# Attention followed by a gated Fourier convolution: head pairs row-tiled, e stationary in 128-column slices, transforms folded twice, casting weight loads

## The chip, the cores and the metric

One Trainium2 chip, one core. The metric is device time in microseconds (us) of the whole launch. The kernel before took 622.55 us (median of 2 runs, 620.84 to 624.26). Engines are called PE (TensorE; PEld is its weight load), DVE (VectorE), ACT (ScalarE), POOL (GpSimd) and SP. A run over 1.5% above the fastest of its kernel counts as slow; only fast runs are compared.

## The reference, cut to what matters

```python
# q, k, v: (8, 12, 448, 64); w_proj: (768, 2304); filter_fft: (448, 768); w_out: (768, 768)
scores = q @ k.T / 8
attn   = exp(scores - m) / (sum(exp(scores - m)) + exp(-m) + 1e-9)     # equals exp(s) / (sum exp(s) + 1), but for the 1e-9
x      = (attn @ v) as (8, 448, 768)
x1, x2, x3 = split(x @ w_proj)
y      = x1 * irfft(rfft(x2, axis=1) * rfft(filter_fft, axis=0)) * x3
out    = y @ w_out
```

Both kernels run the attention of batch b + 1 in the same stretch as the dense part (projections, transform, output) of batch b, so that TensorE has dense matmuls to do while ACT computes exps. The transforms are matmuls with sine and cosine tables.

## The kernel before

One PSUM pool has two buffers each of four tags: `tr` for transposes, `hy` for dense tiles, `sc` for scores, `op` for the attention output. The buffers of one tag form a ring: a new tile gets the buffer of the tile that many places before it, once that one has been read. The parts:

```python
psum = ctx.enter_context(tc.tile_pool(name="psum", bufs=2, space=bass.MemoryType.PSUM))

def attn_pair_scores(A, hp):
    qtps = psum.tile([128, 512], F32, name="qtps", tag="tr")     # q of two heads, transposed; then k
    # ... copies: qT; kTA = k of head 0 over zeros, kTB = zeros over k of head 1
    for i in range(NST):
        for u, kT in enumerate((kTA, kTB)):
            scps = psum.tile([SP, S], F32, name="scps", tag="sc")
            nc.tensor.matmul(scps, kT[:, i * SP : (i + 1) * SP], qT[:, :])
            e = etp.tile([SP, S], BF16, name="ET", tag="ET")
            nc.scalar.activation(e, scps, AF.Exp, scale=SCALE, bias=exp_bias[:SP, 0:1])

def attn_pair_O(A, hp, et):
    for u in range(2):
        oph = psum.tile([SP, NST, DH + 1], F32, name="oph", tag="op")     # two buffers
        # ... 16 matmuls: e in 112-column slices stationary, v and a column of ones moving
        nc.vector.tensor_scalar_add(rec, oph[:, :, DH], 1.0)              # normalisation on DVE
        nc.vector.reciprocal(rec, rec)
        nc.vector.tensor_tensor(xb[:, :, h, :], oph[:, :, 0:DH], ..., op=ALU.mult)

def attn_finish(A):                              # once a batch, behind all six pairs
    for dt in range(NDT):
        xtps = psum.tile([128, 512], F32, name="xtps", tag="tr")
        # ... 4 transposes of xb, one copy to xT[:, dt, :]

# per pair: attn_pair_scores, one chunk of the dense part of the batch before, attn_pair_O
```

The softmax here doesn't subtract the row's maximum and nothing guards it: scores larger than these inputs give would overflow.

## Time and profile before

| | kernel before |
|---|---|
| time | 622.55 us |
| period of the loop (first x1 matmul of a batch to that of the next) | 67.85 us |
| first x1 matmul of batch 0 (the start) | 82.5 us |
| last dense part, to the end | 49.7 us |
| mean granted TensorE clock | 0.988 |

The prediction has 91 us for the start, as it takes two periods of 67.85 us from batch 2; but the first period takes 76.4. It reads the period, the busy times and the groups. One more view matters for what follows: what TensorE does where a pair ends. The columns of a timeline are start (us), length (us), engine, line, operation, count, and in brackets the idle time ahead of it with what ended it.

```profile
244.04 3.76 PE L345 MATMUL pps<-xT,wproj_bf 128*128 128x448 bf16 x19
247.63 1.80 PE L291 MATMUL oph<-vext,ET 112*112 112x65 bf16 x32
249.28 0.36 PE L245 MATMUL qtps<-ident_bf,qf 112*128 112x112 bf16 x4
```

Both heads' outputs run as one row of 32 matmuls, and the next pair's transposes follow at once. No brackets: nothing on TensorE waits for DVE here, although DVE normalises each head. The list of TensorE's waits says nearly the same of the whole run; its columns are us in total, times, and the longest.

```profile
PE fps L156 <- ACT tpages L121: 37.1, 4, 18.1
...
PE xtps L315 <- DVE xb L301: 1.0, 1, 1.0
```

The largest is the sine tables, at the start. For `xb`, the normalised output, it waited once, 1.0 us.

### The profile page before, as it was taken

To read this page: it belongs to the slowest core of one execution; us is meant where nothing else is said; L and a number is where in the kernel's file an instruction comes from. 1 tells how busy PE (TensorE), PEld (TensorE's weight loads), DVE (VectorE), ACT (ScalarE), POOL (GpSimd) and SP (SyncE) were. 2 spreads that over 40 slices of the span, in tenths; PEclk is the share of its full clock that TensorE was granted. 3 is DMA by queue.
4 is the path that set the end of the run, shared out by engine and by line. 5 is a ranking of instruction groups with operands and counts; after the bars stand their busy time and mean duration, and the time that the engine had idled before them with its cause. 6 is when DMAs were issued, how large, how long until landed. Compare 5 with 4: busy or idle time off the path is not lost.

```text
span 615.7 us, 10809 instructions
## 1 busy us (share of the span) xinstructions
PE 541.6 (88%) x4336; PEld 367.8 (60%) x4336; DVE 347.8 (56%) x929; ACT 278.1 (45%) x527; POOL 145.6 (24%) x237
## 2 busy tenths in 40 slices
PE   0127889999999899989999899989999999989977
PEld 0014665766667575757667566757576666757544
DVE  4743545475464935394656746393647546493572
ACT  0106775436436255536355453545453643735112
POOL 3533263033211522033301531052212300100000
PEclk9997898999999999999999999999999999999999
DMA  9999097029900985069900991088901920002002
GB/s 235 235 209 204 1 92 46 1 16 98 113 1 2 79 124 25 2 40 97 91 1 1 91 124 12 1 55 117 56 1 13 101 69 1 1 1 90 2 1 89
DMA packets 137810, 39.04 MB, mean 63 GB/s; under 512 B 131424, under 2 KB 131424, under 8 KB 137760
## 3 DMA queue, kind: packets, MB, share of 16 engines
q0 software_dynamic: 130560, 16.52, 46.6%
q1 hardware_dynamic: 7200, 21.83, 12.0%
q8 instruction: 34, 0.56, 0.4%
q14 instruction: 16, 0.13, 0.1%
HBM read 43.84 MB, written 11.01 MB: 89 GB/s over the span
## 4 chain that ended last, share of the span: by engine, by line
PE 78%; DVE 11%; DMA 6%; ACT 4%; issue 1%; DVEq 0%
PE scps L271 14%; PE oph L291 12%; PE ops L444 10%; PE pps L360 10%; PE pps L345 9%; PE pps L331 9%; PE cps L424 4%; ACT ET L277 4%; DMA w<-in_moe_w_proj_dram 4%; PE xr L378 3%; PE xi L387 3%; DMA f<-in_moe_filter_fft_dram 3%; DVE t L399 2%; PE ktps L255 1%; DVE t L408 1%; PE xtps L315 1%
## 5 line engine op out<-in xcount | busy, mean ns | idle before, releaser
L277 ACT ACTIVATE ET<-scps,exp_bias 112x448 bf16<-112x448 f32 x384 | 217.3, 635 | 214.9 <-PE scps L271 209.3
L291 PEld LDWEIGHTS <-ET 112*112 112x112 bf16 x1536 | 98.0, 133 | 18.1 <-issue 5.3
L291 PE MATMUL oph<-vext,ET 112*112 112x65 bf16 x1536 | 101.8, 217 | 0.7
L299 DVE TENSOR_SCALAR rec<-oph 112x4 f32<-112x4 f32 x96 | 15.2, 158 | 137.4 <-PE oph L291 136.3
L262 POOL MEMSET kTA<- 64x448 bf16 x48 | 22.5, 469 | 236.8 <-PE scps L271 223.0
L444 PE MATMUL ops<-wout_bf,yT 128*112 128x384 bf16 x384 | 74.3, 326 | 0.0
L271 PE MATMUL scps<-qT,kTB 128*112 128x448 bf16 x192 | 69.0, 359 | 4.9 <-DVE kTB L265 2.7
L360 PE MATMUL pps<-wproj_bf,xT 128*112 128x384 bf16 x384 | 72.9, 326 | 0.0
L271 PE MATMUL scps<-qT,kTA 128*112 128x448 bf16 x192 | 69.4, 361 | 3.4 <-DVE kTA L264 1.6
L331 PE MATMUL pps<-xT,wproj_bf 128*128 128x448 bf16 x288 | 71.8, 354 | 0.1
L345 PE MATMUL pps<-xT,wproj_bf 128*128 128x448 bf16 x288 | 64.6, 352 | 0.0
L444 PEld LDWEIGHTS <-yT 128*112 128x112 bf16 x384 | 48.5, 129 | 15.9 <-issue 1.8
L360 PEld LDWEIGHTS <-xT 128*112 128x112 bf16 x384 | 48.6, 129 | 15.7 <-issue 1.5
L424 PE MATMUL cps<-bt,yhat 128*128 128x448 bf16 x192 | 44.9, 351 | 9.2 <-DVE t L408 9.0
L367 ACT CAST x2n<-pps 112x384 bf16<-112x384 f32 x64 | 29.9, 480 | 37.6 <-PE pps L360 37.6
L451 ACT COPY osb<-ops 112x384 f32<-112x384 f32 x64 | 29.8, 480 | 37.1 <-PE ops L444 26.4
L338 DVE CAST x1T<-pps 128x448 bf16<-128x448 f32 x48 | 29.9, 624 | 28.9 <-PE pps L331 28.6
L352 DVE CAST x3T<-pps 128x448 bf16<-128x448 f32 x48 | 30.0, 624 | 23.4 <-PE pps L345 22.3
L345 PEld LDWEIGHTS <-wproj_bf 128*128 128x128 bf16 x288 | 27.9, 98 | 24.8 <-issue 2.8
L301 DVE TENSOR_TENSOR xb<-oph,rec 112x256 bf16<-112x256 f32 x96 | 40.1, 418 | 1.9
L331 PEld LDWEIGHTS <-wproj_bf 128*128 128x128 bf16 x288 | 27.5, 98 | 20.9 <-issue 3.0
L227 POOL DMA_DIRECT2D vext<-in_v_dram x32 | 31.4, 986 | 32.4 <-PE xtps L315 28.2
(68 smaller groups left out, 632.2 us busy)
## 6 DMA issues: line engine op xcount, KB each, us to landing
out_dram<-osb SPq DMA_DIRECT2D x32, 336.0 KB, 2.7
w<-in_moe_w_proj_dram SPq DMA_DIRECT2D x12, 576.0 KB, 7.0
qf<-in_q_dram POOLq DMA_DIRECT2D x32, 168.0 KB, 5.4
kf<-in_k_dram POOLq DMA_DIRECT2D x32, 168.0 KB, 5.2
vext<-in_v_dram POOLq DMA_DIRECT2D x32, 168.0 KB, 6.1
wo<-in_moe_w_out_dram SPq DMA_DIRECT2D x6, 384.0 KB, 5.7
f<-in_moe_filter_fft_dram SPq DMA_DIRECT2D x4, 336.0 KB, 4.6
```

Source lines behind the costliest of these rows:

```text
L227: nc.gpsimd.dma_start(vext[:, st, :, 0:DH], v[b, :, st * SP : (st + 1) * SP, :].rearrange("h p d -> p h d"),)
L271: nc.tensor.matmul(scps, kT[:, i * SP : (i + 1) * SP], qT[:, :],)
L277: nc.scalar.activation(e, scps, AF.Exp, scale=SCALE, bias=exp_bias[:SP, 0:1])
L291: nc.tensor.matmul(oph[:, j, :], et[u][i][:, j * SP : (j + 1) * SP], vext[:, i, h, :], start=(i == 0), stop=(i == NST - 1),)
L301: nc.vector.tensor_tensor(xb[:, :, h, :], oph[:, :, 0:DH], rec[:].unsqueeze(2).to_broadcast([SP, NST, DH]), op=ALU.mult,)
L331: nc.tensor.matmul(pps, wproj_bf[:, kt, dt * 128 : (dt + 1) * 128], xT[:, kt, :], start=(kt == 0), stop=(kt == NDT - 1),)
L338: nc.vector.tensor_copy(hb["x1T"][:, dt, :], pps)
L345: nc.tensor.matmul(pps, wproj_bf[:, kt, 2 * D + dt * 128 : 2 * D + (dt + 1) * 128], xT[:, kt, :], start=(kt == 0), stop=(kt == NDT - 1),)
L352: nc.vector.tensor_copy(hb["x3T"][:, dt, :], pps)
L360: nc.tensor.matmul(pps[:SP, :DCH], xT[:, kt, st * SP : (st + 1) * SP], wproj_bf[:, kt, D + ch * DCH : D + (ch + 1) * DCH], start=(kt == 0) ...
L424: nc.tensor.matmul(cps, yhat[:W, pg, dt * 128 : (dt + 1) * 128], bt[:W, pg, :], start=(pg == 0), stop=(pg == 3),)
L444: nc.tensor.matmul(ops_[:SP, :DCH], yT[:, dt, st * SP : (st + 1) * SP], wout_bf[:, dt, ch * DCH : (ch + 1) * DCH], start=(dt == 0), stop=( ...
```

## The change

The intent is fewer and cheaper TensorE instructions, and an earlier start. Row-tiled means that the scores of two heads, 64 rows each, use the two halves of TensorE's rows, where each head took all 128, half of them zeros. Folded means that sums and differences of mirrored positions and of the two halves of the sequence are formed first, so that the tables shrink. The core of the diff, cut (`...`):

```diff
+    psc = ctx.enter_context(tc.tile_pool(name="psc", bufs=2, space=bass.MemoryType.PSUM))
+    pop = ctx.enter_context(tc.tile_pool(name="pop", bufs=1, space=bass.MemoryType.PSUM))
+    phy = ctx.enter_context(tc.tile_pool(name="phy", bufs=3, space=bass.MemoryType.PSUM))
...
+Q0 = [0, 128, 256, 320]
...  # scores: k of head u lies in rows 64u to 64u+63, no zeros; one exp for both heads
+        tps = phy.tile([128, 512], F32, name="tps", tag="hy")       # transposes of q and k
...
+            sc = psc.tile([SP, 2, 512], F32, name="sc")
+            for u in range(2):
+                r = slice(64 * u, 64 * u + 64)
+                nc.tensor.matmul(
+                    sc[:, u, 0:S], qkT[r, S + j * SP : S + (j + 1) * SP], qkT[r, 0:S]
+                )
+            nc.scalar.activation(e, sc[:, :, 0:S], AF.Exp, scale=SCALE)
...
+    def attn_pair_out(A, hp, et):
+        for u in range(2):
+            op = pop.tile([128, NST, DH + 1], F32, name="op")
...  # 16 matmuls, stationary et[j][:, u, Q0[t] : Q0[t] + 128]; then the same three DVE steps into xb
+        tps = phy.tile([128, 512], F32, name="xps", tag="hy")       # transposes of x, now pair by pair
+        for t in range(NST):
+            nc.tensor.transpose(
+                tb[:, Q0[t] : Q0[t] + 128], xb[:, t, 2 * hp : 2 * hp + 2, :], ident_bf
+            )
+        nc.vector.tensor_copy(xT[:, hp, 0:S], tb[:, 0:S])
...  # dense part: folds of xT on DVE; spectrum 8 matmuls in place of 32; inverse 24 of 224 columns in
...  # place of 24 of 448; every dense tile is phy.tile(..., tag="hy")
-            w32 = stmp_w.tile([128, WCH], F32, name="w32", tag="w32")
-            nc.sync.dma_start(w32, moe_w_proj[...])
-            nc.vector.tensor_copy(wproj_bf[...], w32)
+            nc.gpsimd.dma_start(wproj_bf[:, kt, cs], moe_w_proj[kt * 128 : (kt + 1) * 128, cs])
...
+            for hp in range(NHP):
+                et = attn_pair_scores(N, hp)
+                chunks[hp]()
+                attn_pair_out(N, hp, et)
```

All transposes and all dense tiles now share one ring of three PSUM buffers (`hy`). The x transposes moved from the end of a batch to the end of each pair.

## The prediction

The sum of the period: 51.9 us of work and 6 of waits, so 58, and 525 in all. ACT's "about 40" is 33.5 + 10.2 less a term for the exps of 896 columns. The range of 36 us to each side had one term more, for the mode switches, and the three that are left give 26 in quadrature. Rival 1: the switches cost more than row tiling saves. A mode switch is a change between full-height and row-tiled matmuls on TensorE; as the kernel before has none, the 0.1 us for each is the estimate from the 352 and 189 ns named with it. The "fast load" is the one of 98 ns.

> **What bounds the kernel now.** I read the page's busy shares first, then the chain that ended last in order of time, then the groups of instructions with shapes kept apart, then busy times by stretch, and last the timeline of TensorE inside one batch.
>
> ```profile
> PE 541.6 (88%) x4336; PEld 367.8 (60%) x4336; DVE 347.8 (56%) x929; ACT 278.1 (45%) x527; POOL 145.6 (24%) x237
> ...
> PE 78%; DVE 11%; DMA 6%; ACT 4%; issue 1%; DVEq 0%
> ```
>
> TensorE is busy 88% and carries 78% of the chain. The next view, busy time by stretch, is cut where the projection of x1 recurs in the chain:
>
> ```profile
> 234.01:301.87 67.86, 65.38 (x538) 44.47 (x536) 39.53 (x108) 33.46 (x65) 17.36 (x28) 1.00 0.61 52
> 301.87:369.73 67.86, 65.39 (x538) 44.48 (x536) 39.51 (x108) 33.47 (x65) 17.37 (x28) 1.00 0.57 52
> ```
>
> The columns are the stretch, its length, busy us of PE, PEld, DVE, ACT, POOL, then clock, DMA share and GB/s. One batch takes 67.85 us, PE is busy 65.4 of them at full clock, DVE 39.5 and ACT 33.5. The first x1 matmul of a batch starts at 226.76 us and of the last at 566.03 in the timeline, five periods apart, so the span splits into 91 us before the loop (226.76 minus two periods), 7 x 67.85 = 475 in it, and 49.7 for the last dense part. The launch time of 622.55 is 6.9 over the profiled span.
>
> Busy time hides what a matmul costs, so I price by start-to-start time. These are lines of the chain (start, us, what):
>
> ```profile
> 247.80 1.64 PE oph L291 x32
> ...
> 256.80 3.92 PE pps L360 x24
> ...
> 312.06 3.59 PE pps L345 x19
> ```
>
> 1.64/32 = 51 ns for an attention-output matmul (65 columns streamed), 3.92/24 = 163 ns for 384 columns, 3.59/19 = 189 ns for 448. From the last two, a column costs 0.41 ns with 3 to 5 ns beside; 65 columns should then cost 30 ns, yet they cost 51. The reason is in the groups:
>
> ```profile
> L277 ACT ACTIVATE ET<-scps,exp_bias 112x448 bf16<-112x448 f32 x384 | 217.3, 635 | 214.9 <-PE scps L271 209.3 <-PE oph L291 3.2 <-PE qtps L245 0.5
> ...
> L291 PEld LDWEIGHTS <-ET 112*112 112x112 bf16 x1536 | 98.0, 133 | 18.1 <-issue 5.3 <-ACT ET L277 2.4 <-DVE xb L301 0.9
> ...
> L315 PEld LDWEIGHTS <-xb 112*128 112x128 bf16 x192 | 12.4, 98 | 8.0 <-issue 4.3 <-DVE xb L301 1.1
> ```
>
> A weight load of 112 columns takes 133 ns, one of 128 columns only 98: the wider is faster, and the output matmuls are set by their slow loads. The first line shows ACT waiting for scores, not the other way round.
>
> The budget of a batch by these prices: x1 and x3 72 x 189 ns = 13.6 us; x2 and the output 96 x 163 = 15.6; spectrum 32 x 163 = 5.2; inverse 24 x 189 = 4.5; scores 48 x 189 = 9.1; 72 transposes at 49 ns (four in 0.19 to 0.20 us by the timeline) = 3.5; attention output 192 x 51 = 9.8. Sum 61.3; the other 6.5 are waits (some 2.5 us of idle PE) and small gaps where scores mix with dense matmuls.
>
> [...] Eight exps of 448 run in 4.50 us in the timeline, 0.56 us each[...]. [...] The trace: 550 ns for a 384-column product with PSUM, 350 for a 384-column subtraction in SBUF.
>
> **The change part by part, per batch on TensorE.**
> - Scores: each head contracts 64 rows in place of 128 with zeros. If a pair runs side by side, 24 pairs x 0.19 = 4.6 us in place of 9.1: -4.5. The zero-padded copies of k (a split copy on DVE, two POOL memsets) go as well.
> - Switching: scores of one j are paced by ACT, and dense matmuls fill between, so I expect two mode switches per j, 48 a batch. A recorded 448-column matmul lasts 352 ns and the next starts 189 after it, so up to 0.16 us lies behind the last column; I estimate 0.1 us exposed for each: +4.8.
> - Attention output: e in 128-column slices gets the fast load, so streaming binds, 192 x 31 ns = 6.0 in place of 9.8: -3.8.
> - Forward transform folded twice: 8 matmuls in place of 32: -3.9. Projection of x2 keeps its 48 (now on folded x, 113-column weights hidden behind 384 columns).
> - Inverse: 24 matmuls of 224 columns at about 96 ns in place of 24 x 189: -2.2.
> - Transposes of x take 128 columns: +0.2.
>
> Sum: 61.3 - 4.5 + 4.8 - 3.8 - 3.9 - 2.2 + 0.2 = 51.9, of which 4.8 are switches. The waits I leave at 6: the single buffer for the attention output makes head 1 wait for the normalisation of head 0 (0.16 + 0.18 + 0.42 us of DVE), and three PSUM buffers serve all dense tiles, but DVE has less to do. Period 58 us, 10 less, 69 us over seven batches.
>
> ACT: [...] copies of x1, the transform and the inverse come over (some 8 x 0.48 + 12 x 0.53 = 10.2), so ACT goes from 33.5 to about 40. DVE: the 16 + 8 products and sums of the spectrum (8 x 0.56 on SBUF + 8 x 0.35 = 7.3 against 11.6), the x1 copies and the k copies go, twelve folds of about 0.5 us come: 6.1; in all about 36 against 39.5. Both stay under 58.
>
> Before the loop: now 91 us. Scores start at 51.3 us, behind a serial chain of sine tables and their transposes, with the DMA moving 192 to 239 GB/s in the first 60 us. After the change q, k and v of batch 0 go first, in thirds, so attention 0 runs from some 17 us on under the weight loads. What then binds is bytes: the weights (21.8 MB on the hardware queue less 11.0 of output = 10.8 MB, 46 us at 235 GB/s) and two batches of q, k, v (2.06 MB each as written, at about 120 GB/s when the queue is full in steady state, 17 us each), of which v of batch 1 can come late: about 70 us. -21.
>
> The last dense part: -6.1 of transform matmuls, and the spectrum's waits for DVE partly replaced by waits for folds: about 43 in place of 49.7.
>
> Total: 70 + 7 x 58 + 43 = 519, plus 6.9: 526 us; I say 525.
>
> **The rivals.**
> 1. [...]
> 2. **ACT becomes the bound.** It goes to 40 of 58 us, and it holds both the exps and most PSUM evacuations, in order. [...] Against it: 30% slack, and three buffers of 1 us each.
> 3. **The casting loads are slower or later than thought.** All loads now go through POOL's queue, at 0.93 us of issue for each q, k, v load. The next batch's loads have a full second buffer, so in the loop they are hidden, as the DMA share of 0.6 suggests. At the start it could cost 15 us: loop from 85 us, total 540.
> 4. **Hidden anyway.** If TensorE were not the bound the removed matmuls would be worth nothing. Its 65.4 busy of 67.85 us speaks against it.
>
> **Range and chances.** The terms: [...] waits 6 +- 2.5, so +-18; start +-14; attention output at 31 or 40 ns, +12 at worst. Added in quadrature, about 36 to each side for 8 in 10: 490 to 562. Over 2% faster needs less than 610, beyond everything listed: 0.96. Within 2%: 0.025. Slower: 0.015.
>
> **What would show it.** The period between first x1 matmuls of batches near 58. Two score matmuls of one j starting within a few ns of each other, 24 pairs a batch; if they start 189 apart, the side-by-side step is wrong. [...] Attention-output matmuls 30 to 32 ns apart and their loads near 98 ns; 50 would say that streaming does not bind. Spectrum 8 matmuls, inverse 96 ns each. Exps near 1.0 us long, 24 a batch; ACT busy near 40. First x1 matmul of batch 0 near 70 us. The prediction is wrong if the period stays over 63, with ACT's queue or the switches naming what ended PE's idle time, or if the loop starts after 85 us.

The trace after has these for the prices above. Exps of 896 columns last 0.917 us and follow each other at 0.81 (of 448 columns before: 0.633 and 0.54), and ACT is busy 36.1 us a batch. From the start of an x3 matmul to that of a score pair 297 ns pass, and 326 from a pair to the next x3 matmul (medians, 190 to 635 us), where two full-height matmuls of 448 columns start 189 apart: 0.11 us more ahead of a pair and 0.14 behind it. The x2 matmuls start 163 ns apart, as with 112-column weights before (162), so their 113-column loads of 135 ns are hidden. Products of 768 columns in SBUF take 0.55 to 0.56 us.

## The result, and the profile after

The changed kernel took 680.59 us (median of 2 runs, 679.89 to 681.28) against 622.55: ratio 1.0931, 95% interval 1.0854 to 1.1007, all runs fast. Here and below, a ratio is the mean time of one kernel's fast runs over that of the other's fast runs of the same rounds, so it is not quite the ratio of the medians that I quote. It is slower by 58 us where I had said 98 faster.

| | before | predicted | after |
|---|---|---|---|
| time | 622.55 | 525 | 680.59 |
| start | 82.5 (91 in the prediction) | 70 | 87.9 |
| period | 67.85 | 58 | 78.4 |
| last dense part | 49.7 | 43 | 42.6 |
| clock | 0.988 | not considered | 0.904 |

(After: the first x1 matmuls of batches 0 and 7 start at 87.9 and 636.8 us, seven periods apart; the span is 679.3.) Start and loop are the miss; the last dense part is right. (The clock's record in this run has no entry before 87.4 us, so the 9s at its head say nothing: the 384-column matmuls from 82.34 us on start 0.32 us apart, twice the 163 ns of full clock.) First the page: busy shares, the clock in 40 slices, and the shares of the chain that ended last.

```profile
PE 521.3 (77%) x4112; PEld 315.9 (46%) x4112; DVE 271.3 (40%) x769; ACT 299.2 (44%) x492; POOL 131.3 (19%) x213
...
PEclk9999987889969899698978899698987998688989
...
PE 57%; DVE 15%; ACT 14%; DMA 6%; POOL 4%; issue 3%; ACTq 0%; DVEq 0%; POOLq 0%
```

No engine is full: PE fell from 88% to 77% in a longer span, and nothing else passed 46%. That is the picture of engines that wait for each other. The clock has 6s and 7s all along the loop. One period by engine (the same columns as in the prediction's view by stretch), then the waits of TensorE over the whole run:

```profile
324.77:403.30 78.53, 62.43 (x510) 37.46 (x508) 32.13 (x91) 36.14 (x60) 12.31 (x20) 0.89 0.52 44
```

```profile
PE op L268 <- DVE xb L278: 64.2, 41, 8.0
PE xps L287 <- DVE xb L278: 45.2, 48, 1.6
```

TensorE is idle 16 of 78.5 us of the period. 109 of the 680 us go to waits for `xb`, which were 1.0 us before. The timeline shows where a pair ends, to be set beside the one before:

```profile
330.88 0.65 PE L268 MATMUL op<-vext,e 112*128 112x65 bf16 x16
332.45 0.66 PE L268 MATMUL op<-vext,e 112*128 112x65 bf16 x16 [0.93 <-DVE xb L278]
334.04 0.40 PE L287 MATMUL xps<-ident_bf,xb 128*128 128x128 bf16 x4 [0.93 <-DVE xb L278]
334.27 0.36 PE L239 MATMUL tps<-ident_bf,qf 112*128 112x112 bf16 x4
```

Head 0, wait, head 1, wait, x transposes, and only then the next pair and dense work. The chain that ended last takes each wait apart (start, length, what):

```profile
331.04 0.50 PE op L268 x16
331.54 0.02 issue
331.56 0.17 DVE rec L276
331.73 0.02 issue
331.75 0.19 DVE rec L277
331.94 0.02 issue
331.97 0.44 DVE xb L278
332.40 0.05 issue
332.45 0.68 PE op L268 x16
```

One round trip through DVE is 0.17 + 0.19 + 0.44 us and four hand-overs: 0.93 us seen from TensorE. Twelve a batch make 11.2 us, and in the period above the two waits add up to 6.6 + 5.6 = 12.2 us.

The clock is the second thing. These are stretches of 2 us behind one pair's end; the first number behind the comma is PE's busy time, the third from the end is the clock:

```profile
343.00:345.00 2.00, 0.73 (x19) 0.55 (x16) 1.03 (x5) 0.37 (x1) 0.00 (x0) 1.00 0.00 0
345.00:347.00 2.00, 1.20 (x14) 0.90 (x15) 1.47 (x4) 0.41 (x2) 0.18 (x1) 0.97 0.00 0
347.00:349.00 2.00, 1.89 (x7) 0.71 (x7) 1.56 (x5) 1.74 (x4) 0.00 (x0) 0.50 0.00 0
```

Two round trips leave TensorE 48% busy over 4 us; then the clock halves, for the 10 us to 357, although PE is busy again. Not every pair's end does this: behind the one from 331 to 335 us, 54% busy, the clock stayed whole. No single wait of TensorE from 337 to 347 us is over 0.93 us. In the three periods from 246.7 to 481.8 us the clock was halved for 51.2 of 235.1 us, 17 a batch.

The start: attention 0 was to run from 17 us on without a stop. It has two long waits:

```profile
33.43 1.06 PE L268 MATMUL op<-vext,e 112*128 112x65 bf16 x16 [8.02 <-DVE xb L278]
...
49.74 1.06 PE L268 MATMUL op<-vext,e 112*128 112x65 bf16 x16 [6.53 <-DVE xb L278]
```

DVE's queue has the table work and the sums of the filter ahead of the normalisation, and these wait in turn for POOL (6.75 us until 27.14, for an iota that stands behind the load issues) and for the filter's transfer (7.59 us). These two waits are not the whole of it. The other pairs run as a chain too, 10 us each (first scores at 53.80, 63.88 and 73.94 us), and an experiment below that moves only the x transposes starts at 68.8 us although two such waits, of 7.25 and 4.42 us, stay.

### The profile page after: what moved, and what is told of

Its sections match the earlier page's. It is cut to its first block, busy times and chain, and to the rows that moved or that the text cites. A ratio compares the mean times of both kernels' runs of the same rounds, so it can differ in the third digit from the quotient of the medians.

```text
span 679.3 us, 9984 instructions
## 1 busy us (share of the span) xinstructions
PE 521.3 (77%) x4112; PEld 315.9 (46%) x4112; DVE 271.3 (40%) x769; ACT 299.2 (44%) x492; POOL 131.3 (19%) x213
## 4 chain that ended last, share of the span: by engine, by line
PE 57%; DVE 15%; ACT 14%; DMA 6%; POOL 4%; issue 3%; ACTq 0%; DVEq 0%; POOLq 0%
PE pps L361 10%; ACT e L257 9%; PE pps L324 9%; PE pps L372 8%; PE op L268 7%; PE sc L253 7%; DVE xb L278 5%; DMA out_dram<-osb 4%; PE ops L418 4%; PE xps L287 3%; PE xsp L344 3%; DVE rec L277 2%; ACT cw L400 2%; PE cps L393 2%; DVE rec L276 2%
## 5 line engine op out<-in xcount | busy, mean ns | idle before, releaser
L257 ACT ACTIVATE e<-sc 112x896 bf16<-112x896 f32 x192 | 161.5, 918 | 191.1 <-PE sc L253 190.3
L268 PE MATMUL op<-vext,e 112*128 112x65 bf16 x1536 | 83.1, 203 | 77.5 <-DVE xb L278 64.2
L268 PEld LDWEIGHTS <-e 112*128 112x128 bf16 x1536 | 68.2, 103 | 105.7 <-DVE xb L278 71.6
L253 PE MATMUL sc<-qkT 64*112 64x448 bf16 x384 | 80.9, 458 | 8.6 <-DVE qkT L247 4.3
L324 PE MATMUL pps<-wproj_bf,xf 128*113 128x384 bf16 x384 | 73.8, 335 | 1.2 <-ACT x L369 1.0
L379 DVE TENSOR_TENSOR g<-x,pps 128x448 bf16<-128x448 bf16 x48 | 29.8, 621 | 92.7 <-ACT x L369 68.7
L324 PEld LDWEIGHTS <-xf 128*113 128x113 bf16 x384 | 49.2, 135 | 19.2 <-issue 8.2
L287 PE MATMUL xps<-ident_bf,xb 128*128 128x128 bf16 x192 | 23.3, 257 | 45.2 <-DVE xb L278 45.2
L95 POOL DMA_DIRECT2D qf<-in_q_dram x40 | 34.6, 872 | 69.9 <-PE tps L239 57.1
L278 DVE TENSOR_TENSOR xb<-op,rec 128x256 bf16<-128x256 f32 x96 | 40.7, 424 | 3.3
L345 ACT CAST xs<-xsp 113x384 bf16<-113x384 f32 (+1 forms) x64 | 27.5, 488 | 27.5 <-PE xsp L344 24.1
```

The lines of the kernel that those rows point to most:

```text
L95: nc.gpsimd.dma_start(dst[:, st, h0:h1, 0:DH], src[b, h0:h1, st * SP : (st + 1) * SP, :].rearrange("h p d -> p h d"),)
L253: nc.tensor.matmul(sc[:, u, 0:S], qkT[r, S + j * SP : S + (j + 1) * SP], qkT[r, 0:S])
L257: nc.scalar.activation(e, sc[:, :, 0:S], AF.Exp, scale=SCALE)
L268: nc.tensor.matmul(op[:, t, :], et[j][:, u, Q0[t] : Q0[t] + 128], vext[:, j, h, :], start=(j == 0), stop=(j == NST - 1),)
L278: nc.vector.tensor_tensor(xb[:, :, h, :], op[:, :, 0:DH], rec[:].unsqueeze(2).to_broadcast([128, NST, DH]), op=ALU.mult,)
L287: nc.tensor.transpose(tb[:, Q0[t] : Q0[t] + 128], xb[:, t, 2 * hp : 2 * hp + 2, :], ident_bf)
```

## The experiments

The claims to tell apart: **(1)** the single buffer of the attention output makes the waits; **(2)** the place of the x transposes at the head of the shared ring makes them, as nothing written later gets a PSUM buffer, and so a place in TensorE's order, ahead of them; **(3)** the halved clock, whatever the waits, is the larger part; **(4)** the waits of ACT and its output copies. TensorE's order is not the order of the source: dense matmuls written behind four score steps stand between them in the trace. In the expectations, theory A is claim 2 with the halved clock as its supposed result (that idle time halves it is not shown by itself; measured are 51.2 of 235.1 us at half clock in the changed kernel, and 6.8 of 219.1 with the waits filled), rivals C, E and F are counts of buffers (E is claim 1, F belongs to claim 4), B is the cost of the mode switches, and D that the clock follows something other than idleness. All twelve kernels gave correct results.

### Two buffers for the attention output

```diff
-    pop = ... bufs=1 ...
-    phy = ... bufs=3 ...
+    pop = ... bufs=2 ...
+    phy = ... bufs=2 ...
```

> The changed kernel with two buffers for the attention output and two, not three, for the shared dense ring. Theory A (TensorE waits for two DVE round trips at the end of each pair, and what could fill them is held behind the transposes of x in the shared PSUM ring; the idle time then halves the clock): the wait of the second head's output for xb (6.6 us a batch) goes, the wait of the transposes of x for xb (5.6) stays; period 78.6 to about 69, total about 610 us. Rival B (mode switches of the row-tiled scores are what costs): period stays at 77 to 79, total 670 to 685. Rival C (three dense buffers are too few): worse than 680 with two.

674.69 us (667.84 to 676.37), ratio to before 1.0812 [1.0722, 1.0901]; the changed kernel had 1.0931 [1.0854, 1.1007], so the two are not told apart, and theory A's 610 us was missed. TensorE's waits:

```profile
PE xps L287 <- DVE xb L278: 72.3, 41, 11.0
```

The wait of head 1 is gone from the list, and the x transposes wait 72.3 us in place of 45.2. The end of one pair in its timeline:

```profile
330.05 0.62 PE L268 MATMUL op<-vext,e 112*128 112x65 bf16 x15
331.94 0.40 PE L287 MATMUL xps<-ident_bf,xb 128*128 128x128 bf16 x4 [1.27 <-DVE xb L278]
332.17 0.36 PE L239 MATMUL tps<-ident_bf,qf 112*128 112x112 bf16 x4
```

The transposes still stand right behind the heads, and wait 1.27 us for what DVE has left to do for both. Claim 1 falls: without that wait, the next one takes it up. This run also has one dense buffer fewer, so it tells the worth of the second output buffer only in this arrangement.

### The waits filled with useless matmuls

```diff
+        tps = phy.tile([128, 512], F32, name="xps", tag="hy")     # taken ahead of the heads
         for u in range(2):
...
+            for _ in range(5):
+                nc.tensor.matmul(tps[:, 0:S], et[3][:, u, Q0[3] : Q0[3] + 128], et[3][:, u, :])
```

Five matmuls of 448 columns (5 x 0.19 = 0.95 us) are to run where TensorE would wait 0.93; the transposes overwrite what they leave.

> The changed kernel with five matmuls of 448 columns without use (some 0.95 us) behind each head's output, where TensorE now waits 0.93 us for DVE. Theory A: waits keep their length but the array is never idle, so the clock stays near 1.0 (now 0.89 in the loop) and the period falls from 78.6 by the cold share alone, about 8 us, to 70 to 72; total about 615 to 630. If the clock follows something other than idleness (rival D), it stays near 0.89 and the time rises by some 12 us a batch, to 700 or more.

638.60 us (635.02 to 641.82), ratio 1.0251 [1.0173, 1.0330]: above the kernel before, though by the 2% rule unclear. TensorE did 480 matmuls more, and the kernel became 42 us faster than the changed one. In three middle periods the clock was halved for 6.8 of 219.1 us, and the period fell from 78.4 to 72.6. But the slot of the x transposes is now taken ahead of the heads, and that changed the order too. In four of six pairs the waits keep their length (in the first of a batch head 1 starts 1.62 us after head 0, where it was 1.57), with only the next pair's q transposes let in. In the other two, real work comes between head 1 and its x transposes:

```profile
340.85 0.65 PE L269 MATMUL op<-vext,e 112*128 112x65 bf16 x16
341.43 0.58 PE L253 MATMUL sc<-qkT 64*112 64x448 bf16 x4
341.95 0.55 PE L363 MATMUL pps<-xT,wproj_bf 128*128 128x448 bf16 x2
342.43 0.40 PE L289 MATMUL xps<-ident_bf,xb 128*128 128x128 bf16 x4
```

So the 42 us are not all the clock's, and its price is not isolated. A bound comes from the changed kernel: its loop has 126 us at half clock, which full clock could have made at most 63 shorter. Claim 3 is right that the clock costs something (four x1 matmuls last 1.70 us at 361.98, at half clock, and 0.93 at 373.05), and wrong that it is the larger part of what was lost: with the clock nearly whole in the loop the kernel is still no faster than before.

### A PSUM bank of their own for all transposes

```diff
-    phy = ... bufs=3 ...
+    ptr = ctx.enter_context(tc.tile_pool(name="ptr", bufs=1, space=bass.MemoryType.PSUM))
+    phy = ... bufs=2 ...
-        tps = phy.tile([128, 512], F32, name="tps", tag="hy")
+        tps = ptr.tile([128, 512], F32, name="tps", tag="tr")
-        tps = phy.tile([128, 512], F32, name="xps", tag="hy")
+        tps = ptr.tile([128, 512], F32, name="xps", tag="tr")
```

> The changed kernel with the transposes of attention (q, k and x) in one PSUM bank of their own and two for the dense ring; the attention output keeps its single buffer. Theory A: the order on TensorE can now put dense work into both waits, they nearly vanish, clock near 1.0, period 59 to 63, total 545 to 575. Rival E (the single output buffer alone is the cause): the output wait of 6.6 us a batch stays, period above 70. Rival B: period stays above 72.

602.02 us (600.71 to 604.99), ratio 0.9681 [0.9601, 0.9761]; theory A had said 545 to 575. The source order is that of the changed kernel; only the bank differs. TensorE's order is now:

```profile
334.00 0.66 PE L269 MATMUL op<-vext,e 112*128 112x65 bf16 x16
334.50 0.92 PE L373 MATMUL pps<-xT,wproj_bf 128*128 128x448 bf16 x4
335.26 0.45 PE L394 MATMUL cps<-bt,yh 113*128 113x224 bf16 x3
335.59 0.40 PE L288 MATMUL xps<-ident_bf,xb 128*128 128x128 bf16 x4
```

Dense matmuls stand between head 1 and its transposes, without idle time. One dense buffer fewer, and still 79 us faster than the changed kernel: the shared ring is at the root. The period here is 63 to 68 us (and 97.7 for the first, after an early start at 57.1 us). That two dense buffers are too few is my guess for what is left; no run shows it.

### The same buffers in another order of writing

```diff
-                chunks[hp]()
-                attn_pair_out(N, hp, et)
+                finish(last, queue.pop(0) if queue else [])      # of the pair before
+                last = (N, hp, et)
...
+    def finish(last, pieces):
+        attn_head_out(*last, 0)
+        for p in pieces[:1]: p()
+        attn_head_out(*last, 1)
+        for p in pieces[1:]: p()
+        attn_pair_xT(last[0], last[1])
```

Scores of a pair come first, then the output of the pair before with a piece of dense work behind each head. No buffer changes, and no engine does another number of instructions.

> The changed kernel with all buffers as they are, written in another order: scores of a pair, then the output of head 0 of the pair before, dense work, output of head 1, dense work, transposes of x. Theory A: waits filled without any more buffers, clock near 1.0, period 58 to 62, total 540 to 570, mode switches as many as before. Rival B: no gain beyond a few us, total above 660. Rival E (buffer count): total above 620.

547.55 us (545.47 to 549.57), ratio 0.8791 [0.8729, 0.8853]. The waits for `xb` fall to 24.5 us, 18 of them outside the loop. What is left on top is of claim 4, and the chain shows why, a transfer of the output once in each period:

```profile
PE ops L421 <- ACT osb L428: 14.4, 5, 3.7
```

```profile
254.75 6.74 DMA out_dram<-osb
318.92 5.35 DMA out_dram<-osb
```

The output has two SBUF buffers; the copies of the last two tiles of a batch wait until the first two are in memory, and in ACT's queue they hold up what comes behind.

### With four output buffers

```diff
-    otp = ctx.enter_context(tc.tile_pool(name="otp", bufs=2))
+    otp = ctx.enter_context(tc.tile_pool(name="otp", bufs=4))
```

> The pipelined order of e4 with four buffers for the output rows in place of two; TensorE's order is the same instruction for instruction. In e4 the last output matmuls of each batch wait 4 us for a copy that waits for an output transfer (4 to 7 us beside the loads). If that wait is on the path, the period falls from 63 to 58 or 59 and the total from 547 to about 515 to 522; if other waits take its place, to no less than 540.

525.75 us (525.40 to 526.57), ratio 0.8459 [0.8421, 0.8498], on top of the order above. One period:

```profile
191.66:250.55 58.89, 54.21 (x516) 35.17 (x514) 30.63 (x92) 36.15 (x60) 12.59 (x19) 1.00 0.70 59
```

58.9 us at full clock, as expected; the total is 4 us over the range expected. It does the matmuls and exps of the changed kernel, and the period is within 1 us of what I had predicted for it.

### Four output buffers in the changed kernel alone

The same one-line edit without the new order.

> The changed kernel with four buffers for the output rows and nothing else; TensorE's order is unchanged. The wait for output transfers is 1.8 us of idle TensorE a batch[...]: 2 to 4 us a batch, total 655 to 667. If it were the main cause (rival F: the wait that e5 removed does it all), below 620.

Four runs of 661.15 to 675.14 us, median 673.00. Only the 661.15 counts as fast, since the other three lie over 1.5% above it with a clock of 0.903 to 0.907 against 0.921. The waits for `xb` stay at 65.4 and 45.2 us. The profile is of the fast run: a period of 75.1 us, at a clock of 0.91. What the buffers are worth here is unclear, but no run comes near 620, so they do not mend it.

### Only the x transposes, one pair later

```diff
-    def attn_pair_out(A, hp, et):      # heads, then the x transposes
+    def attn_pair_out(A, hp, et):      # heads only
+    def attn_pair_xT(A, hp):           # the x transposes and their copies
...
                 et = attn_pair_scores(N, hp)
+                if hp == 0:
+                    attn_pair_xT(A, NHP - 1)
                 chunks[hp]()
+                if hp:
+                    attn_pair_xT(N, hp - 1)
                 attn_pair_out(N, hp, et)
```

The outputs of both heads stay written one behind the other, on a single buffer, and the ring stays as it was. If claim 1 had any part left, this kernel would keep the wait of head 1.

> The changed kernel with one thing moved: the transposes of x of a pair are written behind the next pair's scores and dense work; single output buffer and all else kept, the two heads' outputs still written one after the other. Theory A as it stands after e1 and e3 (the transposes of x at the head of the shared PSUM ring hold back everything that could fill both waits): the next pair's transposes, scores and dense work move between the two outputs, both waits nearly vanish, period 62 to 66, total 560 to 600. If the single output buffer were to blame, its wait of 6.6 us a batch stays and the total is above 630.

547.61 us (546.03 to 549.85), ratio 0.8781 [0.8733, 0.8828]: as fast as the full reordering, and better than the 560 to 600 expected. The waits for `xb` are 6.0 and 11.7 us in the whole run, in place of 64.2 and 45.2. The start falls from 87.9 to 68.8 us and the period from 78.4 to 62.4 (mean of seven). TensorE's order:

```profile
265.66 0.65 PE L268 MATMUL op<-vext,e 112*128 112x65 bf16 x16
266.15 0.36 PE L239 MATMUL tps<-ident_bf,qf 112*128 112x112 bf16 x4
...
266.54 0.82 PE L327 MATMUL pps<-wproj_bf,xf 128*113 128x384 bf16 x4
267.24 0.66 PE L268 MATMUL op<-vext,e 112*128 112x65 bf16 x16
```

Between the heads there is now 1.1 us of other work, more than the 0.93 us that the normalisation takes. With the transposes out of the way, the next pair's work moves up by itself. This settles it for claim 2. That it is the PSUM slot and not the order of writing as such that holds work back rests on the run with their own bank, where the source order was kept; how the order is made I have not looked into.

### The smallest mend with four output buffers

The previous kernel with `otp` at 4 buffers.

> The changed kernel with the x transposes of a pair one pair later and four output buffers, the smallest mend. Theory (the place of the x transposes was the cause, the wait for output buffers is the only other one left, and the single buffer for the attention output costs next to nothing once other work lies around it): the 11.6 us that TensorE waits for output copies in the run before it and the tied-up dense buffers go, some 20 us as in the reordered kernel; 525 to 532 us, period 58.5 to 60. Rival (the finer reordering, with dense work between the outputs of the two heads, is worth something by itself): 536 us or more, with TensorE waiting 0.9 us for the normalisation of head 0 in most pairs.

532.75 us (531.97 to 533.66), ratio 0.8586 [0.8559, 0.8614]. It lies between what the two expected. In three periods (190.6 to 370.0 us) head 1 waits for head 0 three times, for 0.6 us in all, so the rival's mechanism is not there. The 7 us to the full reordering are in the loop: 1.8 us in the first period, 0.8 in each of the five middle ones (298.7 against 294.9 us) and 5.2 in the last, part of which its earlier start (69.6 against 73.2 us) and shorter end give back. I did not follow the last period further.

### Row tiling undone

In the reordered kernel with four output buffers, scores as before: k over zeros, 128 rows.

```diff
-                r = slice(64 * u, 64 * u + 64)
-                    sc[:, u, 0:S], qkT[r, S + j * SP : S + (j + 1) * SP], qkT[r, 0:S]
+                    sc[:, u, 0:S], kt2[:, u, j * SP : (j + 1) * SP], qkT[:, 0:S]
```

> e5 with the row tiling undone: each head's k in 128 rows with zeros in the other head's, zeros written once. A pair of scores then costs 2 x 189 = 378 ns in place of the 330 measured with both mode switches, 24 pairs a batch: +1.2 us a batch and 8 to 10 us in all. If mode switches were what costs (rival B), undoing them gains 5 us a batch or more: 35 us less. If the pair gained its full 189 ns with free switches, undoing costs 4.5 us a batch, 32 us.

528.41 us (526.47 to 529.56), ratio 0.8497 [0.8455, 0.8539], against 0.8459 [0.8421, 0.8498] with tiling: 2.7 us by the medians, which these intervals do not tell from none, and less than the 8 to 10 expected. By start-to-start time over four batches, the score lines take 28.2 us with tiling and 39.4 without, 2.8 a batch in favour of tiling. The x1 and x3 matmuls beside them take 63.0 with and 56.1 without, 1.7 a batch against it, and the output matmuls 37.4 and 31.6, 1.4 against it. A gain on its own line is given back on its neighbours' lines. (The 330 of the expectation holds only the switch behind a pair; the one ahead falls on the line before, 297 ns in place of 189 in the trace after.) The edit is not the tiling alone: k is copied head by head, so DVE is busy 33.8 in place of 30.6 us a batch.

### Slices of 112 columns

```diff
-Q0 = [0, 128, 256, 320]
+Q0 = [0, 112, 224, 336]
-                        et[j][:, u, Q0[t] : Q0[t] + 128],
+                        et[j][:, u, Q0[t] : Q0[t] + SP],
```

> e5 with e in 112-column slices again, so weight loads of 112 columns. By the prediction's price (51 in place of 31 ns, 192 a batch) +3.8 us a batch; over eight batches, the first of them less bound by TensorE, 25 to 30 us more than e5. If the outputs hide behind exps and dense waits, under 10 us.

544.75 us (543.80 to 545.70), ratio 0.8758 [0.8709, 0.8807]: 19 us slower than with 128 columns (25 to 30 expected), and the period rises from 59 to 61.3. The x transposes have 112 columns again too, as their input has 112 rows. The weight loads of e (busy us, mean ns), first with 112 columns, then with 128:

```profile
L268 PEld LDWEIGHTS <-e 112*112 112x112 bf16 x1536 | 107.2, 142 | 37.7 <-DVE xb L278 15.5 <-issue 9.7 <-PE op L268 6.3
```

```profile
L268 PEld LDWEIGHTS <-e 112*128 112x128 bf16 x1536 | 67.8, 101 | 40.4 <-DVE xb L278 16.6 <-issue 9.2 <-PE op L268 6.4
```

The load of 128 columns is the faster, as the kernel before had suggested, and over the run it pays 19 us.

### The start: tables first, and the filter first

```diff
-    A = attn_load(0, 3)
     with tc.tile_pool(name="tabs", bufs=1) as tp:
         tables(tp)
+        A = attn_load(0, 3)
+        F = filter_load()          # only in the second of the two kernels
         wproj_load(0)
         wproj_load(1)
-        F = filter_load()          # only in the second of the two kernels
```

> e5 with the tables built ahead of the first loads, so that their POOL steps no longer stand behind 36 load issues and their DVE chain no longer stands between the outputs of attention 0 (waits of 8.0 and 6.5 us in the changed kernel). If these waits set when the loop starts, first dense matmul some 10 us earlier and the total 8 to 12 us under e5; if bytes bind at the start, within 3 us of e5.

> e8 with the filter loaded ahead of the projection weights, since in e8 TensorE still waits 14.8 us at 35 us for a DVE that waits for the filter. If that wait sets the start, first dense matmul 10 us earlier than 69.7 and total 513 to 519; if the loads of batch 1 set it (in e5 and e8 the second batch's dense work starts at the same 132.8 us), total 522 to 527.

526.07 us (525.37 to 526.33), ratio 0.8461 [0.8423, 0.8499], and 524.96 us (524.72 to 525.84), ratio 0.8428 [0.8391, 0.8465], against 525.75 without either. Batch 0 starts at 69.7 and 69.0 us in place of 73.2, but batch 1 at 132.8 and 133.2 as it did (132.8). In the second kernel TensorE waits for batch 1's q and k:

```profile
60.13 0.27 PE L239 MATMUL tps<-ident_bf,qf 112*128 112x112 bf16 x1 [2.55 <-DMA qf<-in_q_dram]
```

A start that comes 4 us earlier meets loads that do not, and gains nothing. The second of these two is the fastest median of all, level with the reordered kernel within what the rounds can tell.

## Why the prediction was wrong

**The step that failed is "The waits I leave at 6".** I carried the idle time of the kernel before over to an order that was made anew. I even named the single buffer "for the attention output" and its 0.16 + 0.18 + 0.42 us of DVE, and did not ask what TensorE would have to do meanwhile. With nothing between, that is 0.93 us or more twice a pair, 12.2 a batch as measured, and 1.8 more in the same period for the output copies: TensorE was idle 16.1 us a batch. The same chain made the start late.

**A term was missing: the clock.** The trace before had a clock of 1.00 in its periods, so every price was a price at full clock. It was halved for 17 us a batch here; what that cost is not isolated (at most 63 us in the loop, and the run with filled waits, whose order changed too, gave 42 back).

Together, in the loop: 7 x (78.4 - 58) = 143 us over the prediction. The run with filled waits got 41 of them back (7 x (78.4 - 72.6)), of which the clock's part is not isolated; the other 102 are near the two waits and the output copies, 7 x (12.2 + 1.8) = 98. The start adds 87.9 - 70 = 18. My 6.9 us of launch over the span was also wrong, as I had set the span of one run against the time of others; in the runs of the changed kernel the difference is 2 us, 5 less. 526 + 143 + 18 - 5 = 682, and 680.59 was measured.

**The buffer I named was the wrong suspect.** A second one moved the wait to the x transposes (674.69 us), and with the transposes one pair later one buffer is enough (547.61). That one buffer does no harm is shown only for an order with work between. What I had not read in the diff is that the x transposes depend on the normalisation of head 1 and hold the next place in the ring that all later work draws from.

**Rivals.** Mode switches were not it: by the trace after, 0.11 us ahead of a score pair and 0.14 behind it (score pair at 327.06, next dense matmul at 327.39), so 0.25 us for two, against the 0.2 that I had put on two; with 24 pairs a batch that is 1.2 us more than foreseen, of the 20 that the period is over. ACT was not the bound; 299 of 679 us busy. The third rival had the loop begin from 85 us, and it did, at 87.9, but not for its reason: with the same loads and the x transposes one pair later it begins at 68.8, near the 70 that I had predicted. "Hidden anyway" is closest: TensorE stopped being the bound, through an order that I had not foreseen.

**What was right.** The work terms. With order and output buffers mended, the same matmuls take a period of 58.9 us (predicted 58) and 525.75 us (predicted 525). The two score matmuls of a pair start 3 ns apart (median of 38 pairs from 190 to 430 us of the changed kernel), so they do run side by side. Output matmuls are 30 ns apart (median; 30 to 32 foreseen) with loads of 101 ns. That price was better than its working: the two lines that it quotes give 0.40 ns a column and 10 beside, so 36 ns for 65 columns, not 30 (with 189 ns for 448 columns, the measured 30 gives 0.415 a column and 3 beside). The score step was put at -4.5 + 4.8 = +0.3 a batch, and undoing it changed nothing measurable. The load of 128 columns (101 ns, against 142 for 112) was put at -3.8 a batch, 27 us over the loop, and is worth 19. Spectrum and inverse, foreseen at 1.3 and 2.3 us a batch, take 2.8 and 3.0 in the reordered kernel. That the total agrees so well is partly luck: the output matmuls, foreseen at 6.0, take 9.3 there with the idle time among them, and the score lines, foreseen at 9.4 with both switches, take 7.0 with the one behind.

## What to carry to other kernels

When a change makes the order anew, price the order: for each TensorE instruction that needs a result of another engine, ask which independent instruction stands between in that ring and queue, and whether it lasts as long as the round trip (here 0.93 us). Let a step that depends on the newest result take its place in a shared ring one round later than the step that makes it. Idle time on TensorE can be paid twice: here short waits that came often (two of 0.93 us a pair) went with a halved clock (51.2 of 235.1 us), and both went when the order was mended (a period of 58.9 us at 1.00 with four output buffers).
